# Gathering slot 1's plain rows between two pairs of stores, and opening its products ahead of the branch

## The chip, the cores and the metric

The kernel runs on one core of a Trainium2 chip. A core has five engines that run side by side: TensorE (PE in the profile, with its weight loads as PEld), VectorE (DVE), ScalarE (ACT), GpSimd (POOL) and SyncE (SP, used here for loads alone). Each engine works through its own list of instructions in order; semaphores make one wait for another. Transfers are issued by POOL (indirect ones, which gather or scatter rows by an index) and by SP, and run on 16 DMA engines. The metric is the device time of one execution, in microseconds (us).

## The reference

The program is chunked attention, followed by a mixture of experts with one expert per token.

```python
# q, k, v: (8, 8, 576, 64); chunks of 64 tokens attend within themselves
scores = scale * q_c @ k_c^T;  attn = softmax(scores);  out = attn @ v_c
x = out.transpose(0, 2, 1, 3).reshape(4608, 512)
# experts: w_gate (512, 8), w1 (8, 512, 1024), w2 (8, 1024, 512)
expert_idx = argmax(x @ w_gate);  gate_w = softmax(x @ w_gate)[expert_idx]
out[mask_e] = gate_w * (relu(x[mask_e] @ w1[e]) @ w2[e])     # for each expert e
```

## The kernel before, in words

The 4608 tokens are 36 tiles of 128 rows. A first part goes through 18 groups of two tiles: scores, softmax, attention output, the gate's logits, and the routing. Routing is done in seven batches of tiles (`BATCHES`, 6, 6, 6, 6, 4, 4, 4). For each batch it works out the place of every row in a scratch tensor in DRAM, `xd`, in which the rows of a batch lie together and are sorted by expert. `store` (line 420) sends each tile there with an indirect transfer on POOL's queue (line 427), through one of twelve views of `xd` that are declared disjoint from one another. A store can be given a tile `after`: then a copy of one column on ACT (line 425) holds it back until that tile is there.

The second part works through "slots". A slot is one expert with 256 plain rows and, by its kind, 0, 64 or 128 extra rows. The kind is only known at run time, so each slot from 1 on begins with a branch (line 1170): `form_a` (line 1116) takes plain rows alone, `form_x` (line 1135) takes extra rows too. A slot's first product is `gemm1` (line 644; matmuls at L616, 256 columns) or, with extra rows, `gemm1_x` (line 618; matmuls at L623, 320 or 384 columns), in eight blocks `f` of twelve matmuls, since each operand is split into a high and a low part and three products of these are summed over four chunks of 128. ACT takes the ReLU (L636, L627), DVE the low part (L641, L630). The second product (L693 to L695) sums three matmuls of 512 columns per block and half.

Rows come to a slot by a gather on POOL's queue, `rows_in` (line 548, the transfer at L550): two transfers of 128 plain rows (`gather`) and one of up to 128 extra rows (`gather_x`, into the tile `xg3`). The first two slots gather early, from the rows of the first batches alone: slot 0 from the first three batches (`TE[0]`, 18 tiles), slot 1 from the first six (`TE[1]`, 32 tiles). The extra rows of slot 1 come from all rows. Gathered rows are transposed on TensorE by `make_xt` (L572) and `make_xt_x` (L605), copied by ACT (L574, L607) and reduced to their low part by DVE (L575, L608).

The framework that builds the program orders any transfer that reads `xd` behind the writes to it that were issued before, and any write behind the reads that were issued before, unless a pair is declared free of dependence. The order of instructions on TensorE, DVE, ACT and POOL is the order in which the program writes them.

Slot 0 has no branch. It is cut into 32 half steps (`BLOCKS`, line 656, and `slot_0`), which `filler(n)` (line 680) hands out one by one between the last steps of the attention part; `halves[0]` counts how many are left, and one last call finishes the slot. At the end of the attention part (lines 1062 to 1093) a loop runs the routing of the last batches, the tables of all slots and a filler for as long as more than five halves are left, and stores one tile per turn. Behind it stand the remaining stores, `gather(1)`, `gather_x(1)`, two weight loads for slot 2 (`load_w`, L532), the fillers up to the last two halves, `make_xt(1)` and the last two halves with slot 0's end. Then each engine loads the kind from memory (L1191, L1193, L1200) and takes the branch of slot 1.

In `form_x` of the slots from 2 on, `FILL` (21) tiny matmuls of eight columns stand between the transposes of the extra rows and the first block. At the start of the program `WARM` (36) matmuls of ones (line 138) run while the first loads are under way. `bank` hands out PSUM banks: "S" alternates between two.

Of the kernel before, what the change touches and what calls it, by code (L numbers as in the profile page):

```python
# [8 lines left out]
F32 = mybir.dt.float32  # L9
F32R = mybir.dt.float32r  # L10
# [8 lines left out]
P = 128  # L19
# [18 lines left out]
NU = SMAX + 2  # L38
XW = D + 16
HB = 3  # L40
WARM = 36
FILL = 21
BIG = 1.0e6

# [2 lines left out]
def attn_moe_kernel(ctx: ExitStack, tc: tile.TileContext, q, k, v, wg, w, out):  # L47
# [50 lines left out]
    def bank(tag, shape):  # L98
        n = 1
        for x in shape[1:]:  # L100
            n *= x
        if tag == "S":
            t = psum[0].tile([P, 512], F32, name="psS", tag="S", bufs=2)
        else:
            t = slots[tag][turns[tag] % len(slots[tag])]
            turns[tag] += 1
        t = t[0:shape[0], 0:n]
        if len(shape) == 3:
            t = t.rearrange("p (a b) -> p a b", b=shape[2])
        return t  # L110
# [22 lines left out]
    ones = const.tile([P, P], BF16, name="ones")  # L133
    nc.vector.memset(ones, 1.0)

    pw = bank("U", [P, P])
    for _ in range(WARM):
        nc.tensor.matmul(pw, ones, ones, start=True, stop=True)
    iota_i = xg[0][0][:, 0:P].bitcast(I32)
    nc.gpsimd.iota(iota_i, pattern=[[1, P]], base=0, channel_multiplier=0)  # L140
    pid_i = xg[0][1][:, 0:NTILE].bitcast(I32)
# [146 lines left out]
        return px  # L288

    stored = set()  # L290

    def x_out(g, px, ri, xt):
        r0 = g * G % RB
# [126 lines left out]
    def store(n, after=None):  # L420

        for k, (b, i, t, di) in enumerate(waiting[:n]):
            x = xb[t // RB % XB][:, t % RB, :]
            if k == 0 and after is not None:
                nc.scalar.copy(x[:, XW - 1:XW], after)
            stored.add(t)
            nc.gpsimd.indirect_dma_start(  # L427
                out=xds[b % 2 * NMAX + i],
                out_offset=bass.IndirectOffsetOnAxis(ap=di[:, i, :], axis=0),
                in_=x, in_offset=None, bounds_check=NT - 1, oob_is_err=False)  # L430
        del waiting[:n]

    active = []
# [113 lines left out]

    def rows_in(t, u, h):
        rows = TE[u] * P if u < 2 and h < 2 else NT
        nc.gpsimd.indirect_dma_start(  # L550
            out=t[:, :], out_offset=None, in_=xd[0:rows, :],
            in_offset=bass.IndirectOffsetOnAxis(ap=place(u, h), axis=0),
            bounds_check=rows - 1, oob_is_err=False)

    def gather(u):
        for h in range(2):
            rows_in(rows_of(u)[h], u, h)
# [53 lines left out]
    def gemm1_pe(par, f, ph, part=range(4)):  # L611
        for kc in part:
            wh = w_hi[par][kc][:, f * 128:(f + 1) * 128]
            wl = w_lo[par][kc][:, f * 128:(f + 1) * 128]
            for i, (a, b) in enumerate(((wh, xhi), (wh, xlo), (wl, xhi))):
                nc.tensor.matmul(ph, a, b[:, kc, 0:BLK], start=kc + i == 0, stop=kc + i == 5)  # L616

    def gemm1_x(par, f, n, hh=None, hl=None):

# [60 lines left out]
    def filler(n):  # L680
        for _ in range(n):
            next(fill, None)
            halves[0] -= 1
# [378 lines left out]
    while active:  # L1062
        for x in "cat":
            advance(x)
        small_op(2)
        pauses()
        side_op(3)
        if halves[0] > 5:
            filler(1)
        if h0:  # L1070
            store(1, h0[-1][0][:, 0:1].bitcast(F32))
    store(NMAX)
    assert len(stored) == NTILE
    gather(1)
    gather_x(1)
    load_w(2, 0)
    load_w(2, 1)
# [10 lines left out]
    xT = y01.rearrange("p a (k t) -> p (a k) t", t=BLK)  # L1088
    hx = ctx.enter_context(tc.tile_pool(name="hx", bufs=HB))
    hq = ctx.enter_context(tc.tile_pool(name="hq", bufs=1))  # L1090
    filler(halves[0] - 2)
    make_xt(1, banks="QK")
    filler(3)
    def slot(u, kd, nxt):
        par = wset(u)
        py = [bank("UV"[m], [P, D]) for m in range(2)]
        if u > 1:
            spread(u + 1)

        last = [[hq.tile([P, BLK], F32R, name=f"{x}{f}") for x in ("hh", "hl")] for f in (6, 7)]  # L1100

        def block(f, h, ms=(0, 1)):
            for m in ms:
                gemm2(par, f, h, m, py)

        def later():

            if u == 1:
                yield from places()
            yield from find_u(u + 3)  # L1110

        def some(x, n):
            for _ in range(n):
                next(x, None)

        def form_a():
            h = []
            x = later()
            for f in range(8):
                h.append(gemm1(par, f, *(last[f - 6] if f > 5 else ())))  # L1120
                if f == 4 and u + 1 < SMAX:

                    tc.mark_branch_hint_location(f"kind{u + 1}", hint=(nxt + 1) >> 1, engines=PE)
                if f == 0 and u > 1:
                    gather_x(u + 1)
                if f == 5 and u > 1:
                    turn()
                    gather(u + 2)
                if f < 7:
                    split_step(u, f)  # L1130
                    some(x, 4 if u == 1 else 1)
                if f > 1:
                    block(f - 2, h[f - 2])

        def form_x(n):

            make_xt_x(u, n)
            pe = bank("K", [n, D])
            if u > 1:
                for _ in range(FILL):  # L1140
                    nc.tensor.matmul(pe[:, 0:8], ones[:, 0:n], ones[:, 0:8], start=True, stop=True)
            h = []
            x = later()

            def more(f):
                gemm2_pe(par, f, *h[f][1], pe)

            for f in range(8):
                h.append(gemm1_x(par, f, n, *(last[f - 6] if f > 5 else ())))
                if f == 4 and u + 1 < SMAX:  # L1150
                    tc.mark_branch_hint_location(f"kind{u + 1}", hint=(nxt + 1) >> 1, engines=PE)
                if f == 0 and u > 1:
                    gather_x(u + 1)
                if f == 5 and u > 1:
                    turn()
                    gather(u + 2)
                if f < 7:
                    split_step(u, f)
                    some(x, 4 if u == 1 else 1)
                if 1 < f < 7:  # L1160
                    block(f - 2, h[f - 2][0])
                    more(f - 2)
            more(5)
            more(6)
            block(5, h[5][0], (0,))
            more(7)
            finish(u, 2, pe, n)
            block(5, h[5][0], (1,))

        with tc.If(kd > 0, label=f"kind{u}") as c:  # L1170
            with tc.If(kd < 2) as c2:
                form_x(EXT // 2)
            with c2.Else():
                form_x(EXT)
        with c.Else():
            form_a()

        nc.gpsimd.drain()
        if u == 1:
            make_xt(u + 1)  # L1180
        else:
            make_xs()
        split_chunk(wset(u + 1), 5)
        for m in range(2):
            for f in (6, 7):
                block(f, last[f - 6], (m,))
            finish(u, m, py[m], on_act=m == 0)

        load_w(u + 2, 2)
# [48 lines left out]
```

## Time and profile before

| | us |
|---|---|
| median of 3 runs | 613.2 |
| lowest and highest | 611.22, 613.5 |
| the profiled execution | 611.45 |
| its span in the trace | 609.7 |

| engine | busy, us | share of the span |
|---|---|---|
| PE | 571.2 | 94% |
| PEld | 500.8 | 82% |
| DVE | 443.1 | 73% |
| ACT | 299.8 | 49% |
| POOL | 256.3 | 42% |

The profile shows one execution. A row of the timeline gives the start and the duration of an instruction (or of several alike), its engine, its line, what it writes and reads, and in brackets how long its engine had stood before it and what released it. A row of the chain gives start, duration and what was worked or waited on. A row of a stretch gives its bounds and length, then for each engine the busy time with the number of instructions in brackets, then the clock that was granted to TensorE (1.00 is full), the busy share of the DMA engines, and GB/s. "POOLq" and the like are the engines' sequencers, which wait on semaphores and issue transfers.

### The profile page before, as it was taken

The numbers are of one execution on the slowest core, as the hardware profiler recorded it, in microseconds if no ns is written. First come the engines' busy times: TensorE is split into PE (matmuls) and PEld (weight loads), VectorE is DVE, ScalarE is ACT, GpSimd is POOL, SyncE is SP. The second block draws the span as 40 slices with busy tenths as digits, with TensorE's granted clock in tenths as the row PEclk, the third lists the DMA queues.
The fourth block names the chain that finished last, engine by engine and source line by source line (L and its number), as shares of the span: only waits on it lengthen the run. The fifth ranks groups of instructions, "written<-read, shape, count | busy, mean of one in ns | idle before, by whom it ended". The sixth has DMA issues, their size and how long they took to land.

```text
span 609.7 us, 14951 instructions
## 1 busy us (share of the span) xinstructions
PE 571.2 (94%) x5710; PEld 500.8 (82%) x5710; DVE 443.1 (73%) x830; ACT 299.8 (49%) x560; POOL 256.3 (42%) x277
## 2 busy tenths in 40 slices
PE   7788879889899999999999989999999999999994
PEld 5566757678699999988788879999998899899893
DVE  6677979987555677776667658778756878878774
ACT  1465656663133545544345435555535555555552
POOL 2113545547524354425253325426432553454252
PEclk9898999999889999999999999999999999999998
DMA  8999999625566263256226512257652235632021
GB/s 282 356 348 309 354 328 308 216 86 197 183 227 204 77 208 109 73 188 217 60 63 223 200 40 81 72 192 275 203 161 85 59 105 198 207 90 82 20 56 37
DMA packets 59875, 103.29 MB, mean 169 GB/s; under 512 B 16416, under 2 KB 32800, under 8 KB 56160
## 3 DMA queue, kind: packets, MB, share of 16 engines
q0 software_dynamic: 20880, 60.74, 29.3%
q1 hardware_dynamic: 38864, 40.94, 21.1%
q8 instruction: 66, 1.08, 0.7%
q14 instruction: 65, 0.53, 0.3%
HBM read 122.65 MB, written 19.96 MB: 234 GB/s over the span
## 4 chain that ended last, share of the span: by engine, by line
PE 80%; DMA 6%; DVE 5%; issue 5%; ACT 2%; POOL 1%; SPq 1%; POOLq 0%; DVEq 0%; ACTq 0%
PE psS L616 18%; PE psS L623 8%; PE psL L616 6%; PE psU L693 5%; PE psU L694 5%; PE psV L693 5%; PE psU L695 5%; PE psV L694 5%; PE psV L695 5%; DMA out_y<-y,oid 3%; PE psL L623 3%; PE psU L286 2%; PE psS L232 2%; PE psT L309 2%; PE psL L321 1%
## 5 line engine op out<-in xcount | busy, mean ns | idle before, releaser
L77 DVE TENSOR_TENSOR wlo<-raw,whi 128x1024 fp32r<-128x1024 f32 x134 | 163.8, 1222 | 26.6 <-ACT whi L76 24.2
L76 ACT CAST whi<-raw 128x1024 fp32r<-128x1024 f32 x134 | 140.2, 1046 | 0.1
L532 POOL DMA_INDIRECT raw<-in_w,widx x71 | 78.8, 1109 | 124.0 <-DVE wlo L77 54.5
L636 ACT ACTIVATE hh<-psS 128x256 fp32r<-128x256 f32 x110 | 42.5, 386 | 174.1 <-PE psS L616 115.1
L616 PE MATMUL psS<-xhi,whi 128*128 128x256 f32 x344 | 97.6, 284 | 1.4 <-PE psV L695 1.2
L616 PE MATMUL psS<-xlo,whi 128*128 128x256 f32 x344 | 97.4, 283 | 0.3 <-DVE xlo L575 0.3
L616 PE MATMUL psS<-xhi,wlo 128*128 128x256 f32 x344 | 97.3, 283 | 0.0
L703 POOL DMA_INDIRECT out_y<-y,oid x40 | 46.8, 1171 | 115.5 <-ACT y L700 32.2
L641 DVE SCALAR_TENSOR_TENSOR hl<-psS,hh 128x256 fp32r<-128x256 f32 x110 | 46.4, 422 | 63.5 <-ACT xh L627 31.8
L550 POOL DMA_INDIRECT xg<-xd,idx x58 | 65.7, 1132 | 21.6 <-issue 18.4
L616 PEld LDWEIGHTS psS<-xhi,whi 128*128 128x128 f32 x344 | 65.7, 191 | 5.8 <-issue 2.4
L616 PEld LDWEIGHTS psS<-xlo,whi 128*128 128x128 f32 x344 | 65.7, 191 | 3.1 <-DVE xlo L575 0.5
L616 PEld LDWEIGHTS psS<-xhi,wlo 128*128 128x128 f32 x344 | 65.7, 191 | 0.0
L693 PE MATMUL psU<-whi,hh 128*128 128x512 f32 x144 | 57.6, 400 | 2.5 <-issue 1.3
L694 PE MATMUL psU<-wlo,hh 128*128 128x512 f32 x144 | 57.2, 397 | 0.0
L693 PE MATMUL psV<-whi,hh 128*128 128x512 f32 x144 | 56.9, 395 | 0.0
L694 PE MATMUL psV<-wlo,hh 128*128 128x512 f32 x144 | 56.7, 394 | 0.0
L695 PE MATMUL psU<-whi,hl 128*128 128x512 f32 x144 | 56.4, 392 | 0.0
L695 PE MATMUL psV<-whi,hl 128*128 128x512 f32 x144 | 56.4, 391 | 0.0
L84 POOL TENSOR_TENSOR wlo<-raw,whi 128x512 fp32r<-128x512 f32 x16 | 20.3, 1271 | 66.2 <-ACT whi L83 55.7
L427 POOL DMA_INDIRECT xd<-xb,di x32 | 32.3, 1008 | 14.7 <-issue 4.4
L594 DVE STREAM_TRANSPOSE y<-xg 128x1024 f32<-128x1024 f32 x16 | 33.1, 2070 | 0.6
(236 smaller groups left out, 1198.2 us busy)
## 6 DMA issues: line engine op xcount, KB each, us to landing
kb<-in_k SPq DMA_DIRECT2D x36, 256.0 KB
qt<-in_q SPq DMA_DIRECT2D x36, 256.0 KB
vb<-in_v SPq DMA_DIRECT2D x36, 256.0 KB
xg<-xg SPq DMA_DIRECT2D x256, 32.0 KB
raw<-in_w SPq DMA_DIRECT2D x16, 256.0 KB
raw<-in_w,widx POOLq DMA_INDIRECT x71
xg<-xd,idx POOLq DMA_INDIRECT x58
out_y<-y,oid POOLq DMA_INDIRECT x40
```

The costliest lines, as they stand in the source:

```text
L76: nc.scalar.copy(hi, src)
L77: nc.vector.tensor_tensor(lo, src, hi.bitcast(F32), ALU.subtract)
L532: nc.gpsimd.indirect_dma_start(out=raw[c][:, :], out_offset=None, in_=w, in_offset=bass.IndirectOffsetOnAxis(ap=widx[:, u, c:c + 1], axis= ...
L550: nc.gpsimd.indirect_dma_start(out=t[:, :], out_offset=None, in_=xd[0:rows, :], in_offset=bass.IndirectOffsetOnAxis(ap=place(u, h), axis=0 ...
L616: nc.tensor.matmul(ph, a, b[:, kc, 0:BLK], start=kc + i == 0, stop=kc + i == 5)
L623: nc.tensor.matmul(ph, a[par][kc][:, f * 128:(f + 1) * 128], b[:, kc, 0:BLK + n], start=kc + i == 0, stop=kc + i == 5)
L636: nc.scalar.activation(hh, ph, AF.Relu)
L641: nc.vector.scalar_tensor_tensor(hl, ph, 0.0, hh.bitcast(F32), ALU.max, ALU.subtract)
L693: nc.tensor.matmul(py, hh, wh, start=f == 0, stop=False)
L694: nc.tensor.matmul(py, hh, wl, start=False, stop=False)
L695: nc.tensor.matmul(py, hl, wh, start=False, stop=f == 7)
L703: nc.gpsimd.indirect_dma_start(out=outs[m], out_offset=bass.IndirectOffsetOnAxis(ap=oid[u % 3][0:n, m:m + 1], axis=0), in_=y, in_offset=No ...
```

## The change

Four things are changed. The warm-up is done with 9 matmuls of 512 columns in place of 36 of 128. The loop at the end of the attention part no longer stores tiles of the last batch; behind the loop all but the last two tiles are stored, then `gather(1)` is issued, then the last two tiles are stored, without the ACT copy; `gather(1)` is declared free of dependence on those stores of the last batch that were issued before it. One more half of slot 0 stands behind `make_xt(1)`. And slot 1's blocks 0 and 1 of the plain rows (`ahead`, two calls of `gemm1`) are issued ahead of the branch; in `form_x` their extra rows then have a product of their own, `gemm1_xx`, with 64 or 128 columns. `form_a` of slot 1 gets 27 of the tiny matmuls at its start, which the other form already has in the later slots and still lacks in slot 1.

```diff
-WARM = 36
+WARM = 9
...
-    pw = bank("U", [P, P])
+    pw = bank("U", [P, 4, P])
     for _ in range(WARM):
-        nc.tensor.matmul(pw, ones, ones, start=True, stop=True)
+        nc.tensor.matmul(pw, ones, ones.unsqueeze(1).broadcast_to([P, 4, P]), start=True, stop=True)
...
     stored = set()
+    late = []
...
-            nc.gpsimd.indirect_dma_start(
+            s = nc.gpsimd.indirect_dma_start(
                 out=xds[b % 2 * NMAX + i],
                 out_offset=bass.IndirectOffsetOnAxis(ap=di[:, i, :], axis=0),
                 in_=x, in_offset=None, bounds_check=NT - 1, oob_is_err=False)
+            if t >= TE[1]:
+                late.append(s)
...
     def rows_in(t, u, h):
         rows = TE[u] * P if u < 2 and h < 2 else NT
-        nc.gpsimd.indirect_dma_start(
+        g = nc.gpsimd.indirect_dma_start(
             out=t[:, :], out_offset=None, in_=xd[0:rows, :],
             in_offset=bass.IndirectOffsetOnAxis(ap=place(u, h), axis=0),
             bounds_check=rows - 1, oob_is_err=False)
+        if u == 1 and h < 2:
+
+            for s in late:
+                tc.declare_no_dep(g.ins, s.ins, reason="these rows lie behind the ones gathered")
...
+    def gemm1_xx(par, f, n):
+
+        ph = bank("S", [P, n])
+        for i, (a, b) in enumerate(((w_hi, xhi), (w_lo, xhi), (w_hi, xlo))):
+            for kc in range(4):
+                nc.tensor.matmul(ph, a[par][kc][:, f * 128:(f + 1) * 128], b[:, kc, BLK:BLK + n],
+                                 start=kc + i == 0, stop=kc + i == 5)
+        xh = hx.tile([P, EXT], F32R, name="xh")[:, 0:n]
+        nc.scalar.activation(xh, ph, AF.Relu)
+        xl = hx.tile([P, EXT], F32R, name="xl")[:, 0:n]
+        nc.vector.scalar_tensor_tensor(xl, ph, 0.0, xh.bitcast(F32), ALU.max, ALU.subtract)
+        return xh, xl
...
-        if h0:
+        if h0 and waiting and waiting[0][0] < NBAT - 1:
             store(1, h0[-1][0][:, 0:1].bitcast(F32))
-    store(NMAX)
+    store(len(waiting) - 2)
+    gather(1)
+    store(2)
     assert len(stored) == NTILE
-    gather(1)
     gather_x(1)
     load_w(2, 0)
     load_w(2, 1)
...
-    filler(halves[0] - 2)
+    filler(halves[0] - 3)
     make_xt(1, banks="QK")
-    filler(3)
+    filler(4)
...
+        ahead = [gemm1(par, f) for f in range(2)] if u == 1 else []
...
+        def fill_up(to, n):
+
+            for _ in range(n):
+                nc.tensor.matmul(to[:, 0:8], ones[:, 0:to.shape[0]], ones[:, 0:8], start=True, stop=True)
+
         def form_a():
+            if u == 1:
+                fill_up(bank("K", [P, D]), 27)
...
-                h.append(gemm1(par, f, *(last[f - 6] if f > 5 else ())))
+                h.append(ahead[f] if f < len(ahead) else gemm1(par, f, *(last[f - 6] if f > 5 else ())))
...
             if u > 1:
-                for _ in range(FILL):
-                    nc.tensor.matmul(pe[:, 0:8], ones[:, 0:n], ones[:, 0:8], start=True, stop=True)
+                fill_up(pe, FILL)
...
-                h.append(gemm1_x(par, f, n, *(last[f - 6] if f > 5 else ())))
+                h.append((ahead[f], gemm1_xx(par, f, n)) if f < len(ahead)
+                         else gemm1_x(par, f, n, *(last[f - 6] if f > 5 else ())))
```

## The prediction

> **What bounds the kernel now.** I read the page's head and its chain first, then TensorE's instructions in order of time, the granted clock in short stretches, and last POOL's instructions and the chain around the first branch.
>
> ```profile
> span 609.7 us, 14951 instructions
> PE 571.2 (94%) x5710; PEld 500.8 (82%) x5710; DVE 443.1 (73%) x830; ACT 299.8 (49%) x560; POOL 256.3 (42%) x277
> PE 80%; DMA 6%; DVE 5%; issue 5%; ACT 2%; POOL 1%; SPq 1%; POOLq 0%; DVEq 0%; ACTq 0%
> ```
>
> TensorE is busy for 94% of the span and 80% of the chain that ended last. A change pays if it takes away time in which TensorE stands, or in which it runs at a low clock. The change works at one such place, the passage from slot 0 to slot 1.
>
> ```profile
> 159.14 0.39 PE L693 MATMUL psV<-whi,hh 128*128 128x512 f32 x1
> ...
> 161.40 0.75 PE L572 MATMUL psQ<-ident,xg 128*128 128x128 f32 x4 [1.42 <-DMA xg<-xd,idx]
> 163.12 1.13 PE L572 MATMUL psK<-ident,xg 128*128 128x128 f32 x4 [0.97 <-DMA xg<-xd,idx]
> ...
> 168.34 1.65 PE L623 MATMUL psS<-xhi,whi 128*128 128x384 f32 x4 [0.68 <-ACT xhi L607]
> ...
> 174.61 0.85 PE L623 MATMUL psL<-xhi,whi 128*128 128x384 f32 x4
> ```
>
> TensorE waits 1.42 us for the first gather of slot 1, 0.97 us for the second and 0.68 us for ACT's copy of the transposed extra rows: 3.07 us. The arm taken is the one with 128 extra rows (384 columns at L623). The start of its third block, 174.61, is the mark against which I sum, since nothing behind it is changed.
>
> ```profile
> 53.19:56.60 3.41, 1.69 (x39) 1.59 (x32) 3.38 (x5) 0.44 (x5) 2.74 (x6) 1.00 1.02 358
> 83.90:87.32 3.42, 1.96 (x15) 1.58 (x15) 2.45 (x7) 1.30 (x3) 1.63 (x3) 1.00 1.00 332
> 159.00:162.41 3.41, 1.73 (x9) 1.04 (x7) 0.00 (x0) 0.22 (x1) 2.54 (x3) 1.00 0.50 120
> 162.41:165.82 3.41, 2.70 (x9) 2.32 (x10) 1.73 (x7) 0.95 (x2) 1.46 (x2) 0.50 0.78 250
> 165.82:169.24 3.42, 2.74 (x10) 2.05 (x9) 1.98 (x4) 0.59 (x1) 2.03 (x2) 0.50 0.99 395
> 169.24:172.66 3.42, 3.42 (x12) 3.42 (x11) 0.15 (x3) 0.02 (x1) 1.18 (x2) 0.50 0.52 201
> 172.66:176.07 3.41, 3.41 (x21) 3.41 (x21) 1.94 (x9) 1.09 (x4) 0.88 (x1) 1.00 0.92 288
> ```
>
> Here the second number is TensorE's busy time and the third from the end the granted clock. The clock changes on a grid of 3.41 us. After a stretch with 1.73 us of work (159.00) it is halved; a stretch with 1.96 us (83.90) was held. It comes back only behind a full stretch (3.42, from 169.24): 2.70 and 2.74 us were too little. So three stretches run at half clock, and their 2.70 + 2.74 + 3.42 = 8.86 us of work cost about 4.4 us more than at full clock. With the 3.07 us of waits the passage loses 7.5 us, which is all that a perfect change could win here.
>
> **What the change does, part by part.** *The warm-up.* 36 products of 128 columns become 9 of 512, the same 4608 columns.
>
> ```profile
> 1.05 4.02 PE L138 MATMUL psU<-ones 128*128 128x128 bf16 x36 [1.05 <-DVE ones L134]
> ...
> 7.28 0.69 PE L232 MATMUL psS<-kb,qt 64*64 64x64 f32 x32 [1.31 <-DMA qt<-in_q]
> ```
>
> They end at 5.07, and the scores then stand for a load until 7.28. Up to 2 us in the length of the warm-up are covered by that load: nothing, and without this cover 4.02 us at most.
>
> *The stores and the gathers on POOL's queue.* Before, the four stores of the last batch go first, then both plain gathers, the extra one and the weight loads.
>
> ```profile
> 149.74 0.98 POOL L427 DMA_INDIRECT xd<-xb,di  x1 [0.15 <-POOL xb L406]
> 151.03 1.37 POOL L427 DMA_INDIRECT xd<-xb,di  x1 [0.30 <-issue]
> 152.70 0.97 POOL L427 DMA_INDIRECT xd<-xb,di  x1 [0.30 <-issue]
> 153.98 1.20 POOL L427 DMA_INDIRECT xd<-xb,di  x1 [0.30 <-issue]
> 157.92 1.04 POOL L550 DMA_INDIRECT xg<-xd,idx  x1 [2.74 <-PE psS L616]
> 159.26 1.01 POOL L550 DMA_INDIRECT xg<-xd,idx  x1 [0.30 <-issue]
> 160.58 1.00 POOL L550 DMA_INDIRECT xg<-xd,idx  x1 [0.30 <-issue]
> 161.88 0.99 POOL L532 DMA_INDIRECT raw<-in_w,widx  x1 [0.30 <-issue]
> ```
>
> After, the order is store, store, gather, gather, store, store, extra gather, loads. The gathers no longer wait for the last batch, so the first takes about the place of the third store: 152.8, and the second 154.15 (1.34 us apart, as 157.92 and 159.26).
>
> ```profile
> 153.98 2.97 DMA xd<-xb,di
> ...
> 159.26 3.81 DMA xg<-xd,idx
> ...
> 167.70 0.60 ACT xhi L607
> ...
> 174.77 2.08 PE psL L623 x12
> 176.85 0.23 PE psU L693
> ```
>
> They land 3.48 us (157.92 to 161.40) and 3.81 us behind their starts, at 156.3 and 157.96, ahead of TensorE's need at 159.14. Both waits, 2.39 us, go.
>
> What is late next: the two stores behind the gathers. The edit frees each gather of the stores already in the list `late`; the two stores that are issued afterwards write the same scratch tensor that the gathers read, and nothing frees them. The trace shows such a pair, slot 0's gathers and the store behind them.
>
> ```profile
> 118.21 1.05 POOL L550 DMA_INDIRECT xg<-xd,idx  x1 [0.16 <-PE psT L277]
> 119.56 1.01 POOL L550 DMA_INDIRECT xg<-xd,idx  x1 [0.30 <-PE psT L309]
> ...
> 124.17 1.05 POOL L427 DMA_INDIRECT xd<-xg,di  x1 [3.16 <-DVE xb L298]
> ```
>
> ```profile
> L427 POOLq EVENT_SEMAPHORE  x2: 43/43/43, 121.8 to 123.4; - x2
> ```
>
> That store's two semaphore waits end at 121.8 and 123.4, which is 3.6 and 3.8 us behind the starts of the two gathers, their landing; the store starts 0.75 us later. The releaser that the row names, L298, I put down to chance. So the third store starts at 157.96 + 0.75 = 158.7 and the fourth at 160.0 (1.28 later, as 152.70 and 153.98). It lands at 162.97 (2.97). The extra gather, which reads all rows, waits for it and starts 0.97 later (156.95 to 157.92) at 163.9. It lands 3.5 to 3.8 us on; I take 167.5. Queued behind on POOL are the loads for slot 2, at 165.2 in place of 161.88. Their data are first needed behind the third block, past 174, which covers 3.4 us; uncovered they would cost those 3.4 us.
>
> The four one-column ACT copies that paced these stores go away; ACT is not what TensorE waits for there, so nothing.
>
> *The order on TensorE.* One more half of slot 0 (three products of 512 columns) lies behind the transposes, and two blocks of slot 1's plain rows go ahead of the branch.
>
> ```profile
> 139.24 0.60 PE L309 MATMUL psT<-ident,xb 128*128 128x128 f32 x4
> 139.68 0.60 PE L309 MATMUL psQ<-ident,xb 128*128 128x128 f32 x4
> 140.12 0.51 PE L931 MATMUL psL<-sel_g,lp 128*128 128x8 f32 x4
> ...
> 164.91 0.69 DVE L575 TENSOR_TENSOR xlo<-psK,xhi 128x512 fp32r<-128x512 f32 x1 [1.28 <-ACT xhi L574]
> ...
> 204.92 2.87 PE psS L616 x24
> ```
>
> From 159.14: eight transposes at full clock 0.88 (139.24 to 140.12), to 160.02; three halves of 3 x 0.23, 2.07, to 162.09. Under these halves ACT makes two copies (0.60 each) and DVE two differences (0.69 each), done near 161.8: no wait. Two plain blocks take 2.87 (204.92), to 164.96. TensorE's sequencer crosses the branch under these 2.87 us of products; uncovered it would at first only eat into the wait that follows. Then TensorE stands until 167.5, for 2.5 us; transposes 0.6, ACT's copy with its hand-over 0.66 (as now): 168.8.
>
> Then come the extra rows of the two blocks, 24 products of 128 columns. No row shows this shape. From below, a third of 384 columns is 0.058 us each (2.08 for 12), 1.4 in all; from above, as much as 256 columns, 0.12 each, 2.9. I take 0.11, the spacing of the 128-column transposes above, which load as large a weight for as few columns: 2.64, to 171.4. (So splitting the two blocks costs 2.87 + 2.64 against 2 x 2.08 = 4.16, that is 1.35 us more work.) By the Trainium skill, TensorE: Matmul & The Clock Gate, section LDWEIGHTS, a weight load takes its columns divided by 1.2 GHz, an estimate of 107 ns however short the product; by it the split would be 0.1 us cheaper. No run here shows it for this shape.
>
> *The clock.* The waits of 2.5 and 0.66 us lie within 3.8 us. For nearly every position of the grid one stretch of 3.41 us then holds under 1.73 us of work, and the clock is halved. It returns behind one full stretch, or two where the first is partly idle. Stepping the grid through its positions, with the clock halved behind less than 1.9 us of work (between 1.73 and 1.96) and given back behind a stretch with less than 0.5 us of idle time, the loss behind 168.8 is 1.4 to 3.1 us, 2.2 in the mean. The third block then starts at 173.6, against 174.61.
>
> **Sum.** Waits 3.07 - 3.16 = -0.1; half clock 4.4 - 2.2 = 2.2 gained; more work -1.35; and 0.25 that these terms leave open of the 15.47 us from 159.14 to 174.61 before: a gain of 1.0 us. The profiled execution took 611.45 us, 1.75 over its span; it becomes 610.45. The median of the three runs, 613.2, lies 1.75 above it; the same gain gives **612.2 us**. As behind the mark TensorE runs on without a break for most of the time, the shift passes to the end.
>
> **The rivals.** 0.5% of the time, 3.1 us, is about what a measurement of this kernel can tell from no change.
>
> *A, the forecast:* the last two stores wait for the gathers, TensorE waits for the extra rows and cools. 612.2, own range 610.2 to 614.6 (the ends of the half-clock loss, of the 24 products, and grids on which the kernel before loses less than the 10.2 us at half clock seen here). Chance 0.60.
>
> *B, the stores are not held.* Then they start at 155.5 and 156.8, the fourth lands at 159.8, the extra gather starts at 160.7 and lands by 164.5, before 164.96. Only 0.66 us of wait stays, the clock holds, the third block starts at 168.9, and the gain is 5.7: 607.5. For it: the edit says that the rows lie apart, and the row of the store at 124.17 names L298, a write to another tile, as its releaser. Against it: the semaphore rows. Chance 0.14.
>
> *C, the clock holds in spite of the wait.* Then 171.4, a gain of 3.2: 610.0. For it: 1.96 us of work in a stretch held the clock. Against it: 1.73 did not, and there the longest single wait was 1.42 us, shorter than the new one. The Trainium skill, same page, section Why this matters for your kernels, asks only that no gap exceed about 3 us; by that rule the 2.5 us would be harmless and C the outcome, but the trace, with the clock halved at 162.41 behind 1.42 us and a part of the next wait, speaks against it. Chance 0.12.
>
> *D, slower: the narrow products don't bring the clock back.* They give TensorE 128 columns in 0.11 us where a plain block gives it 256 in 0.12. If a stretch of them counts as too little work, as 2.70 us did, they run at half clock for all of 5.3 us, and one or two stretches behind them too: a loss of 2.64 + 1.7 = 4.3 to 2.64 + 3.4 = 6.0 in place of 2.2. The mark moves to 175.7 or 177.4, and the time to 614.3 or 616.0. It decides from a half-clock loss of 3.2 us on. For it: two stretches with four fifths of work stayed at half clock. Against it: the scores' small products (L232) do not cool it. Chance 0.14.
>
> **How the numbers follow.** Faster by over 0.5%: all of B, three quarters of C, 0.04 of A: 0.27. Slower by over 0.5%: about half of D and 0.03 of A: 0.10. The rest, 0.63, is within 0.5%. The range holds A and C whole, B at its edge and the lower part of D: 607.4 to 615.2.
>
> **What the profile will show.** Right: the first gathers start near 152.8 and 154.2, the next store near 158.7, the extra gather near 163.9; TensorE has no wait for the plain rows, two blocks of L616 end near 165.0, and a wait of about 2.5 us for the extra gather follows; the 24 narrow products are 0.11 us apart at full clock; the clock is halved once, for one or two stretches. The prediction is wrong if the third store starts near 155.5 (B), if the granted clock stays at 1.00 through the wait (C), or if the narrow products and what follows run at 0.50 for over two stretches (D); and in its size if the extra gather lands a microsecond earlier or later, for each such microsecond moves the mark by as much and can decide over the clock.

## The result, and the profile after

| | before | after |
|---|---|---|
| median, us (22 runs each) | 614.42 | 619.15 |
| lowest and highest, us | 610.32, 622.03 | 616.11, 623.5 |
| ratio after to before | | 1.0087 [1.0063, 1.0112] |
| profiled execution, us | 611.45 | 616.83 |

The change made the kernel slower by 0.87%, some 5.3 us (0.0087 x 614.42), where 612.2 us was forecast, with a chance of 0.63 for a difference within 0.5%. Here and below the median is over all executions of a run, while a ratio leaves out those that are more than 1.5% above the fastest of their kernel, which changes a reading for the cut kernels alone. The head of the page of after:

```profile
span 615.0 us, 14931 instructions
PE 578.0 (94%) x5707; PEld 503.6 (82%) x5707; DVE 440.6 (72%) x830; ACT 298.6 (49%) x556; POOL 265.3 (43%) x277
```

TensorE is busy for 6.8 us more (571.2 before) at the same share, so the clock and the waits are the places to look, not another engine. In POOL's instructions of after (start, duration, line; in brackets the idle time ahead and what ended it) the order and the hold are as forecast, 2 to 3 us later:

```profile
154.18 0.97 POOL L428 DMA_INDIRECT xd<-xb,di  x1 [0.30 <-issue]
155.46 1.05 POOL L553 DMA_INDIRECT xg<-xd,idx  x1 [0.30 <-issue]
156.81 1.01 POOL L553 DMA_INDIRECT xg<-xd,idx  x1 [0.30 <-issue]
161.05 1.02 POOL L428 DMA_INDIRECT xd<-xb,di  x1 [3.24 <-DMA xg<-xd,idx]
162.38 1.00 POOL L428 DMA_INDIRECT xd<-xb,di  x1 [0.31 <-issue]
165.96 1.05 POOL L553 DMA_INDIRECT xg<-xd,idx  x1 [2.58 <-DVE o_b L893]
```

The third store stands 3.24 us for the gathers, and the extra gather starts at 165.96. TensorE in the passage (L579 are the transposes of slot 1's plain rows, L612 of the extra rows, L630 the narrow products, L643 the third block):

```profile
168.90 0.63 PE L579 MATMUL psQ<-ident,xg 128*128 128x128 f32 x4
...
174.80 0.65 PE L612 MATMUL psT<-ident,xg 128*128 128x128 f32 x4
...
176.46 0.67 PE L630 MATMUL psS<-xhi,whi 128*128 128x128 f32 x4 [1.01 <-ACT xhi L614]
...
179.20 0.91 PE L643 MATMUL psL<-xhi,whi 128*128 128x384 f32 x4
```

The mark, the third block, is 4.6 us later than before (174.61). But here nothing waits for the extra rows: the plain transposes themselves start only at 168.90, where 159.14 was assumed. The reason stands in ACT's instructions ahead of them, and in the stretches of the clock (length, TensorE's busy time, and third from the end the granted clock):

```profile
152.02 0.18 ACT L411 ACTIVATE ce<-psK 128x8 f32<-128x8 f32 x1
158.97 0.66 ACT L656 ACTIVATE hh<-psS 128x256 fp32r<-128x256 f32 x2 [6.77 <-remote]
```

```profile
155.45:158.86 3.41, 1.73 (x5) 0.86 (x5) 0.00 (x0) 0.00 (x0) 2.05 (x2) 1.00 0.58 170
158.86:162.27 3.41, 2.40 (x11) 2.40 (x12) 2.65 (x11) 0.66 (x2) 1.02 (x1) 0.50 0.08 27
```

ACT does nothing for 6.77 us, though the products that it is to take were ready (the first of them ended near 151). TensorE has four stops of 0.28 to 0.84 us in that time for which the trace names no releaser, and then stands 1.29 us for what follows ACT. This came in this one execution: in the 17 other traces that reach slot 1, ACT never stands for over 2.5 us in the 20 us ahead of its transposes, and two of them (f2 and w2) are of the same kernel and slower than before all the same. So it can't be what makes 22 runs slower. A single profile would have led to the wrong cause here; the experiments had to tell.

### The profile page after: what moved, and what is told of

Read it like the earlier page. It is cut to its first block, busy times and chain, and to the rows that moved or that the text cites. A ratio compares the mean times of both kernels' runs of the same rounds, so it can differ in the third digit from the quotient of the medians.

```text
span 615.0 us, 14931 instructions
## 1 busy us (share of the span) xinstructions
PE 578.0 (94%) x5707; PEld 503.6 (82%) x5707; DVE 440.6 (72%) x830; ACT 298.6 (49%) x556; POOL 265.3 (43%) x277
## 5 line engine op out<-in xcount | busy, mean ns | idle before, releaser
L535 POOL DMA_INDIRECT raw<-in_w,widx x71 | 84.6, 1191 | 121.2 <-DVE wlo L77 39.9
L623 PE MATMUL psS<-xhi,whi 128*128 128x256 f32 x352 | 100.8, 286 | 2.4 <-DVE hl L661 1.3
L623 PE MATMUL psS<-xlo,whi 128*128 128x256 f32 x352 | 100.3, 285 | 0.3 <-DVE xlo L582 0.3
L623 PE MATMUL psS<-xhi,wlo 128*128 128x256 f32 x352 | 100.2, 285 | 0.3 <-issue 0.3
L553 POOL DMA_INDIRECT xg<-xd,idx x58 | 68.3, 1178 | 25.3 <-issue 21.9
L623 PEld LDWEIGHTS psS<-xhi,whi 128*128 128x128 f32 x352 | 67.9, 193 | 7.9 <-issue 2.5
L623 PEld LDWEIGHTS psS<-xlo,whi 128*128 128x128 f32 x352 | 67.9, 193 | 3.2 <-DVE xlo L582 0.5
L623 PEld LDWEIGHTS psS<-xhi,wlo 128*128 128x128 f32 x352 | 67.9, 193 | 0.5 <-issue 0.5
```

What stands on the lines that cost most here:

```text
L535: nc.gpsimd.indirect_dma_start(out=raw[c][:, :], out_offset=None, in_=w, in_offset=bass.IndirectOffsetOnAxis(ap=widx[:, u, c:c + 1], axis= ...
L553: g = nc.gpsimd.indirect_dma_start(out=t[:, :], out_offset=None, in_=xd[0:rows, :], in_offset=bass.IndirectOffsetOnAxis(ap=place(u, h), ax ...
```

## The experiments

All kernels were run next to the kernel before; each ratio is to that, with its 95% interval. The four cut kernels are not in the table. "Passage" is from slot 0's transposes to slot 2's (before: 129.39 to 201.07, 71.68 us), "half clock" the time at 0.50 inside it.

| run | stores held by the gathers | median, us | ratio | passage, us | half clock, us |
|---|---|---|---|---|---|
| the kernel after, as above | yes | 619.15 | 1.0087 [1.0063, 1.0112] | 74.68 | 6.83 |
| f2, the kernel after | yes | 613.39 | 1.0051 [1.0020, 1.0082] | 68.60 | 0 |
| w2, the kernel after | yes | 615.63 | 1.0079 [1.0055, 1.0104] | 73.34 | 10.24 |
| f4, old warm-up, instructions level | yes | 614.04 | 1.0061 [1.0029, 1.0094] | 68.77 | 0 |
| e2, old warm-up | yes | 618.36 | 1.0100 [1.0052, 1.0148] | 73.47 | 10.24 |
| e4, no blocks ahead | yes | 616.25 | 1.0070 [1.0030, 1.0111] | 73.83 | 6.83 |
| w1, narrow products made wide | yes | 612.89 | 1.0044 [1.0011, 1.0076] | 70.46 | 3.41 |
| h1, the wait filled with products | yes | 611.15 | 1.0014 [0.9987, 1.0041] | 68.87 | 0 |
| h3, stores freed | no | 610.80 | 1.0013 [0.9982, 1.0045] | 67.51 | 0 |
| h6, stores freed, no blocks ahead | no | 612.73 | 1.0013 [0.9979, 1.0048] | 70.45 | 3.41 |
| e3, stores first | no | 613.21 | 1.0011 [0.9977, 1.0046] | 71.88 | 6.83 |
| f3, stores first, no blocks ahead | no | 610.21 | 0.9999 [0.9972, 1.0025] | 66.90 | 0 |
| e1, before with the new warm-up | as before | 614.76 | 1.0047 [1.0014, 1.0080] | 69.34 | 3.41 |
| f1, the same, instructions level | as before | 610.80 | 1.0000 [0.9968, 1.0033] | 69.78 | 0 |
| h5, the kernel before | as before | 612.19 | 1.0028 [0.9999, 1.0058] | 69.38 | 0 |

h5 sets the scale: two equal kernels came out 0.28% apart, so no single difference below that is read. Passage and half clock are of one execution each.

**The warm-up (e1, e2, f1, f4).** e1 puts the new warm-up alone into the kernel before, e2 puts the old one back into the kernel after:

```diff
-WARM = 9
+WARM = 36
...
-    pw = bank("U", [P, 4, P])
+    pw = bank("U", [P, P])
     for _ in range(WARM):
-        nc.tensor.matmul(pw, ones, ones.unsqueeze(1).broadcast_to([P, 4, P]), start=True, stop=True)
+        nc.tensor.matmul(pw, ones, ones, start=True, stop=True)
```

> The kernel before with the new warm-up alone (9 products of 512 columns for 36 of 128). Theory 1 (the loss lies ahead of slot 1's passage and comes from TensorE's instruction stream being 27 products shorter from the start, so that every later instruction lies elsewhere in the blocks in which instructions are fetched): slower than before by 5 to 10 us, ratio 1.008 to 1.016; slot 0's transposes near 131.6 in place of 129.39 and the start of slot 1's transposes near 166 to 169 in place of 160. Theory 2 (the loss comes from the stores and gathers moved on POOL's queue, or the ACT copies taken away): ratio 1.000 within 0.003. Theory 3 (it comes from the blocks put ahead of the branch): ratio 1.000 within 0.003.

> The kernel after with the old warm-up back, all the rest kept. Theory 1: the passage keeps its gain of about 5 us and the loss ahead of it goes: ratio to before 0.990 to 0.995, slot 0's transposes near 129.4 and slot 1's third block near 169. Theories 2 and 3: as the kernel after, ratio 1.006 to 1.011.

The warm-up alone cost 0.47%, less than theory 1 asked for and more than the other two allow; but with the old one back the kernel after was no faster (1.0100). The two then differ in how many instructions stand ahead of all later ones. f1 adds 27 tiny products to e1's warm-up, f4 takes the 27 out of `form_a` of e2, so that both have the number of the kernel before:

```diff
+    for _ in range(27):
+        nc.tensor.matmul(pw[:, 0, 0:8], ones, ones[:, 0:8], start=True, stop=True)
```

> The kernel before with the new warm-up and 27 tiny products of 8 columns behind it, so that TensorE has as many instructions as before and all later ones lie where they lay. If the warm-up alone costs time because the later instructions lie elsewhere (theory 1): ratio to before 1.000 within 0.003. If it costs by its own length or shape: as the run with the new warm-up alone, 1.003 to 1.008.

> The kernel after with the old warm-up, and without the 27 tiny products in the arm that is not taken, so that all instructions behind the arms lie where they lay in the kernel before. Theory H: as the kernel after, ratio 1.006 to 1.011. Theory 1 (the warm-up's shift ahead of the passage costs 3 us): 1.001 to 1.006.

f1 is at 1.0000, f4 with 1.0061 where the kernel after is (1.0051 in f2, run beside it). So the new warm-up costs nothing where the later instructions keep their place, and it is not what made the kernel after slower. Theory 1 falls as the cause; that the place of the instructions is what cost e1 its 0.47% is argued from f1 alone, and the intervals of the two overlap.

**The hold, and the blocks ahead (e3, e4, f2, f3).** e3 stores all four tiles first and leaves the gathers freed; e4 takes out the two blocks ahead of the branch; f3 does both; f2 is the kernel after again.

```diff
-    store(len(waiting) - 2)
+    store(len(waiting))
     gather(1)
-    store(2)
```

```diff
-        ahead = [gemm1(par, f) for f in range(2)] if u == 1 else []
+        ahead = []
```

> The kernel after with all four last stores ahead of the two gathers, which stay freed of them, so that no store is held by a gather. Theory 1: as the kernel after within 0.003 (ratio 1.006 to 1.011), since nothing waited for the held stores there. Theory 2: if the gathers' place between the stores costs the time ahead of the passage, 5 to 10 us faster than the kernel after, ratio 0.993 to 1.001; if the missing ACT copies cost it, as the kernel after. Theory 3: as the kernel after.

> The kernel after without the two blocks ahead of the branch (slot 1 computes all its blocks 384 columns wide again). Theory 1: the time ahead of the passage stays as in the kernel after (slot 1's transposes near 169), and the passage loses 0.5 to 3 us for the wait for the extra rows that the two blocks covered, less 1.3 us for narrow products that are gone: ratio to before 1.006 to 1.013. Theory 2: the same. Theory 3: ratio 1.000 or below.

> The kernel after once more. Theory H (the hold: the last two stores wait for the gathers, the extra gather comes late, TensorE stands about 2 us for it and then runs two to three stretches at half clock): ratio 1.006 to 1.011, ACT without its stop of 6.8 us near 152 to 159 (an accident of that execution), a wait of about 2 us for the extra rows, the third block 14.5 to 16 us behind the start of slot 1's transposes. If the stop of ACT belongs to the kernel, it is there again.

> All four last stores ahead of the freed gathers, and no blocks ahead of the branch: all blocks 384 columns wide. Theory H: neither the hold nor the wait is there, TensorE has no gap over 0.7 us in the passage, the clock stays, and the third block starts 9 to 11 us behind the start of slot 1's transposes (15.5 before): 4 to 6 us faster than before, ratio 0.990 to 0.994. Theory 3 (the blocks ahead cost nothing of their own): the same as the run with the stores first and the blocks ahead, 1.001.

Theory 3 falls with e4: without the blocks ahead it is still 0.70% slower. With the stores first the loss is gone, with the blocks ahead (1.0011) and without them (0.9999). f2, the kernel after, is at 1.0051, a little under the 1.006 expected; ACT's long stop is not there, and TensorE stands for the extra rows:

```profile
165.55 0.75 PE L612 MATMUL psT<-ident,xg 128*128 128x128 f32 x4 [1.51 <-DMA xg<-xd,idx]
```

But in f2's trace the clock held, so the third block starts 11.73 us behind slot 1's transposes and not 14.5 to 16. f3 was expected to win 4 to 6 us and won nothing, though its passage is 3.1 us shorter than the mean of the four traces with the stores and gathers of before (70.0); that stays open. In e3 TensorE stops in the narrow products behind the branch, and the trace names no releaser:

```profile
172.15 0.90 PE L630 MATMUL psS<-xlo,whi 128*128 128x128 f32 x3 [1.89 <-issue]
```

That is not of e3 alone: the kernel before has such a stop in slot 1's second block where it keeps its clock (1.31 us in f1, 1.22 in h5).

**Cut kernels (c0, c1).** To see where along the program the time is lost, both kernels were cut behind slot 0 and behind slot 1, so that these times are of parts of the computation.

> The kernel before cut behind slot 0: slot 1 and all later slots, the extra gather of slot 1 and the weight loads for slot 2 are left out; the stores and the two plain gathers stay. It measures the part ahead of the passage alone, near 167 us (slot 0 ends near 161 in the profile, then the scaling and the store of its rows), run after run. Only its difference to the kernel after cut at the same place counts.

> The kernel after cut behind slot 0 in the same way. Theory H (all of the loss is in the passage: the wait for the extra rows and the half clock behind it): as the kernel before cut there, within 1 us. Theory U (the part ahead of the passage got slower, as the profiles with slot 0's transposes at 130.5 to 136 hint against 129.4 before): 2 to 5 us longer.

> The kernel before cut behind slot 1 (slots 2 and later are left out, everything up to slot 1's last products, stores and the weight loads issued there is kept): near 215 us. Only its difference to the kernel after cut there counts.

> The kernel after cut behind slot 1. Theory H: 3 to 5 us longer than the kernel before cut there, with none of it ahead of the passage. Theory U: the same 3 to 5 us here, and 2 to 5 of them already in the pair cut behind slot 0. Theory L (the loss comes behind slot 1, from the later weight loads): within 1 us of the kernel before cut there.

By the medians, all executions counted, behind slot 0: 166.8 us before (163.49 to 167.74, 7) against 167.64 after (165.24 to 170.81, 6); behind slot 1: 219.59 (215.95 to 221.42, 7) against 219.27 (218.8 to 221.63, 5). By the ratios, which are to the whole kernel before (610.6 us), it looks otherwise: 0.2681 [0.2666, 0.2696] against 0.2720 [0.2702, 0.2738] behind slot 0 and 0.3542 [0.3522, 0.3561] against 0.3609 [0.3589, 0.3630] behind slot 1, which is 2.4 and 4.1 us longer and what theory U says. But they rest on 3 executions against 3 and 3 against 5, picked by a line through a spread of some 4 us that is as large as what was looked for. So the cut kernels are inconclusive, with a hint at theory U. The spread shows in the other traces too, where slot 0's transposes start between 128.22 and 136.18 in kernels with the change and between 129.29 and 132.39 in those without, and at 135.63 in the kernel before cut behind slot 1.

**The hold alone (h3, h6), and its wait filled (h1).** h3 keeps the order on POOL and frees the last stores of the gathers as well, which makes rival B real; h6 takes out the blocks ahead too. h1 keeps the hold and has TensorE do 7 products on the ones where it would stand.

```diff
-    late = []
+    late, early_g = [], []
...
             if t >= TE[1]:
                 late.append(s)
+                for g in early_g:
+                    tc.declare_no_dep(s.ins, g.ins, reason="these rows lie behind the ones gathered")
...
         if u == 1 and h < 2:
+            early_g.append(g)
```

```diff
-                fill_up(bank("K", [P, D]), 27)
+                fill_up(bank("K", [P, D]), 13)
...
+            pe = bank("K", [n, D])
+            if u == 1:
+                for _ in range(7):
+                    nc.tensor.matmul(pe.rearrange("p (a t) -> p a t", t=P), ones[:, 0:n], ones.unsqueeze(1).broadcast_to([P, 4, P]), start=True, stop=True)
             make_xt_x(u, n)
-            pe = bank("K", [n, D])
```

> The kernel after with the last two stores freed of the gathers as well, so that the order on POOL stays and only the hold goes (rival B made real). Theory H: the third store starts about 1.3 us behind the second gather, the extra gather about 160 to 161 on the old time axis, TensorE's wait for the extra rows is under 0.5 us, and the ratio to before falls to 0.990 to 1.002, 3 to 6 us below the kernel after. If the order itself (the gathers between the stores) is the cost: as the kernel after, 1.005 to 1.009.

> The same without the two blocks ahead of the branch. Theory H: no wait for plain rows, at most 1 us for the extra ones, no half clock in the passage: ratio 0.990 to 1.000. If the freed order costs by itself: 1.005 to 1.009.

> The kernel after with the hold, and 7 products of 512 columns on the ones (1.6 us, their result is not used) where TensorE stands for the extra rows; 14 of the tiny products in the arm not taken are left out, so that later instructions lie where they lay. If the half clock behind the wait is what the hold costs: the passage stays at full clock in most executions, ratio 0.997 to 1.003. If the hold costs by something else (later weight loads, the wait itself): as the kernel after, 1.005 to 1.009.

> The kernel before once more: ratio 1.000 within 0.003. Its trace shows whether the wait for the two gathers (2.4 us) and the three stretches at half clock come in each execution; if the stretches are missing, the profile on which the prediction's 4.4 us for the half clock rested was one of the dear ones.

POOL's instructions of h3:

```profile
153.88 1.17 POOL L555 DMA_INDIRECT xg<-xd,idx  x1 [0.30 <-issue]
155.35 1.11 POOL L428 DMA_INDIRECT xd<-xb,di  x1 [0.30 <-issue]
156.77 1.00 POOL L428 DMA_INDIRECT xd<-xb,di  x1 [0.31 <-issue]
160.34 1.05 POOL L555 DMA_INDIRECT xg<-xd,idx  x1 [2.58 <-DMA xd<-xb,di]
```

The store starts 1.47 us behind the gather (4.24 in after), the extra gather at 160.34, close to the 160.7 forecast for rival B, and no wait for the extra rows is left. The ratio is 1.0013. In h6 TensorE, without the blocks ahead, still stands 2.00 us for the extra rows (1 us at most was expected) and has one stretch at half clock; its ratio is 1.0013 all the same. h1 keeps the hold, as the third store's wait of 3.05 us shows, but not TensorE's idle time:

```profile
164.84 1.69 PE L1169 MATMUL psK<-ones 128*128 128x512 bf16 x7
166.81 0.75 PE L612 MATMUL psT<-ident,xg 128*128 128x128 f32 x4 [0.29 <-DMA xg<-xd,idx]
168.23 0.66 PE L630 MATMUL psS<-xhi,whi 128*128 128x128 f32 x4 [0.68 <-ACT xhi L614]
...
170.97 0.92 PE L643 MATMUL psL<-xhi,whi 128*128 128x384 f32 x4
```

It takes no wait away, since the products take as long as TensorE stood; and still the ratio is 1.0014. Its interval lies apart from those of w2 and of the result, but overlaps with that of f2. So the order of the transfers is not the cost, nor the time for which the extra rows are late, nor the later weight loads behind them: it is that TensorE stands there. What is left is what standing does to the clock.

**Why the half clock is dear here (w1, w2).** w1 makes the 24 narrow products 256 columns wide; w2 is the kernel after beside it.

```diff
-        ph = bank("S", [P, n])
+        pw = bank("S", [P, BLK])
+        ph = pw[:, BLK - n:BLK]
-                nc.tensor.matmul(ph, a[par][kc][:, f * 128:(f + 1) * 128], b[:, kc, BLK:BLK + n],
+                nc.tensor.matmul(pw, a[par][kc][:, f * 128:(f + 1) * 128], b[:, kc, n:BLK + n],
```

> The kernel after with the extra rows' 24 products of the first two blocks computed over 256 columns (the second half of the plain rows along with the 128 extra ones; the plain part is thrown away, the result is the same). 24 products of 0.12 in place of 0.114 us: 0.15 us more at full clock. If it is the narrow products that don't bring the clock back (rival D): where the clock is halved it is for one or two stretches, none of them a full one without return, and the ratio falls to 1.002 to 1.005. If their width doesn't matter: as the kernel after, 1.005 to 1.010.

> The kernel after once more, beside the run with the wide products: ratio to before 1.005 to 1.009; if its trace has the clock halved in the passage, for two to three stretches, with a full stretch of narrow products that stays at half.

TensorE's instructions of w2, and its clock stretch by stretch:

```profile
159.87 0.63 PE L579 MATMUL psQ<-ident,xg 128*128 128x128 f32 x4
...
167.88 1.13 PE L612 MATMUL psT<-ident,xg 128*128 128x128 f32 x4 [1.94 <-DMA xg<-xd,idx]
...
169.68 1.12 PE L630 MATMUL psS<-xhi,whi 128*128 128x128 f32 x4 [0.68 <-ACT xhi L614]
...
174.86 1.59 PE L643 MATMUL psL<-xhi,whi 128*128 128x384 f32 x4
...
203.48 0.63 PE L579 MATMUL psT<-ident,xg 128*128 128x128 f32 x4
```

```profile
164.57:167.98 3.41, 1.47 (x13) 1.26 (x12) 0.85 (x2) 0.73 (x2) 2.51 (x3) 1.00 0.49 125
167.98:171.39 3.41, 2.73 (x12) 2.33 (x13) 0.82 (x3) 0.58 (x1) 2.79 (x3) 0.50 1.00 329
171.39:174.81 3.42, 3.42 (x18) 3.42 (x18) 0.99 (x5) 0.28 (x1) 1.30 (x2) 0.50 0.92 326
174.81:178.22 3.41, 3.41 (x13) 3.41 (x13) 1.49 (x5) 0.28 (x1) 0.00 (x0) 0.50 1.03 428
```

The wait of 1.94 us leaves 1.47 us of work in a stretch, and the clock is halved. The stretch from 171.39 holds nothing but narrow products, without a gap, and the clock does not return; only behind the stretch from 174.81, which holds the third block, is it back. 2.73 + 3.42 + 3.41 = 9.56 us of work at half clock cost 4.8 us. Two more traces have such a stretch, e2 with narrow products up to 180.97 and the kernel after cut behind slot 1 with narrow ones up to 171.63:

```profile
177.65:181.07 3.42, 3.42 (x18) 3.42 (x17) 0.98 (x5) 0.28 (x1) 1.54 (x2) 0.50 0.90 298
168.86:172.27 3.41, 3.41 (x17) 3.41 (x17) 1.07 (x6) 0.55 (x2) 2.24 (x2) 0.50 0.85 258
```

Both are followed by another at half clock. The stretches of w1:

```profile
165.08:168.49 3.41, 1.55 (x10) 1.36 (x11) 1.13 (x4) 0.58 (x1) 2.49 (x4) 1.00 0.90 260
168.49:171.91 3.42, 3.42 (x18) 3.42 (x17) 0.98 (x5) 0.28 (x1) 2.61 (x3) 0.50 0.96 309
171.91:175.32 3.41, 3.41 (x20) 3.24 (x20) 1.74 (x6) 0.99 (x4) 0.00 (x0) 1.00 1.00 394
```

Halved in the same way (1.55), but one full stretch of wide products brings the clock back: 3.41 us at half in place of 10.24, and a passage of 70.46 against 73.34. Of the two stretches that w1 is spared, one is due to the width. The other is the first of w2, which has a gap of 0.68 us in it and would not have been full with wide products either; that is where the grid fell. By this reading the narrow products' own part in w2 is one stretch, 1.7 us of the 4.8. The ratios (1.0044 and 1.0079) go the same way, with intervals that overlap.

**The clock of the timed executions.** A trace shows one execution, but every timed one has its mean granted clock on record. One minus this clock, times the span, is the most that half clock can have cost it. The means over the executions that count for the ratio:

| run | lost to the clock, us | before, beside it | difference | measured loss, us |
|---|---|---|---|---|
| w2, the kernel after | 13.2 | 8.9 | 4.3 | 4.8 |
| f2, the kernel after | 11.6 | 10.0 | 1.6 | 3.1 |
| f4, old warm-up, instructions level | 13.0 | 10.0 | 3.0 | 3.7 |
| e2, old warm-up | 15.5 | 11.3 | 4.2 | 6.1 |
| e4, no blocks ahead | 12.3 | 11.3 | 1.0 | 4.3 |
| w1, narrow products made wide | 9.4 | 8.9 | 0.5 | 2.7 |
| h1, the wait filled | 9.4 | 9.0 | 0.4 | 0.9 |
| h3, stores freed | 11.1 | 9.0 | 2.1 | 0.8 |
| h5, the kernel before | 10.7 | 9.0 | 1.7 | 1.7 |

The measured loss is the ratio less one, times the median of the kernel before. In the five runs left out here (e1, e3, f1, f3, h6) the difference lies between 1.2 us less than before and 0.8 more. By h5 a difference is good to some 2 us. In w2, f4 and e2 the clock can account for most of the loss, and in h1 its extra loss is gone. In f2, e4 and w1 it accounts for about half or less, and the rest was not found. These means don't say where in the program the clock was low.

## Why the prediction was wrong

**Right:** POOL's queue. With the passage of w2 starting 0.73 us later than forecast (159.87 for 159.14): second gather 154.77 (154.15 forecast), third store 158.91 (158.7), extra gather 164.02 (163.9), its rows there at 167.88 (167.5). The wait is 1.94 us (2.5), ACT's hand-over 0.68 (0.66). The 24 narrow products take 2.74 us at full clock (176.46 to 179.20 in after) against 2.64. Their 0.114 us each fits, to 7%, the estimate of 107 ns from the Trainium skill, TensorE: Matmul & The Clock Gate, section LDWEIGHTS. The plain rows are no longer waited for.

**The failed step: the term of the half clock, on both sides of the sum.** It was entered as 4.4 us before less 2.2 after, a gain of 2.2. By the mean clock of the timed executions, over the whole program, it is a loss of 1.6 us in f2 and 4.3 in w2.

On the side of before, 4.4 us was the price of one execution, and was taken for that of the kernel. Three more traces of the same passage (f1, e1, h5) have 0, 3.41 and 0 us at half clock, for waits as long. h5:

```profile
164.35 0.75 PE L572 MATMUL psQ<-ident,xg 128*128 128x128 f32 x4 [1.38 <-DMA xg<-xd,idx]
...
166.16 0.75 PE L572 MATMUL psK<-ident,xg 128*128 128x128 f32 x4 [1.05 <-DMA xg<-xd,idx]
...
169.63 0.96 PE L623 MATMUL psS<-xhi,whi 128*128 128x384 f32 x4 [0.68 <-ACT xhi L607]
```

```profile
161.60:165.03 3.43, 2.05 (x11) 1.36 (x9) 0.00 (x0) 0.00 (x0) 2.51 (x4) 1.00 0.40 106
165.03:168.44 3.41, 2.36 (x13) 1.76 (x13) 1.70 (x7) 1.17 (x2) 1.87 (x2) 1.00 0.85 232
```

Here the grid splits the two waits so that 2.05 and 2.36 us of work stay, and the clock holds. From the end of the 29 halves to the mark these kernels take 15.47 (on record), 13.57, 13.13 and 13.17 us, 13.8 in the mean: 1.6 us of the forecast gain were only the bad draw of one profile. The saving from a held clock is also smaller than 4.4 us, since f1 and h5 then have the stop without a releaser of 1.31 and 1.22 us. For after the grid was stepped through its positions; for before it was not, although the range of the forecast names such executions.

On the side of after, "It returns behind one full stretch" was read from a stretch of wide products and applied to narrow ones. It fails there, so that in the executions of w2 and e2 the 2.2 us became 4.8; in those of f2 and f4 they became nothing, since the clock held. By the Trainium skill, same page, section Part 1: The HAM clock gate (the "warmup" mystery), one sustained busy window of about 3.4 us brings the full clock back; w2, e2 and the kernel after cut behind slot 1 each have such a window, full by the profile, behind which it did not. That page's remark that the window runs free of the kernel fits the spread between executions of one kernel.

**A second step fell with it:** "nothing behind it is changed", said of the mark. In w2 the half clock reaches past the mark, and from there to slot 2's transposes it takes 28.62 us (174.86 to 203.48) against 26.46 in all four traces of before. Without half clock, in f2, it is 27.11: of the 0.65 us more, 0.09 lie in the third block and the rest in two short stops in the last halves ahead of slot 2's transposes, whose cause is open. The sum had nothing for them.

**The sum again,** from the end of 29 halves to slot 2's transposes: 13.8 + 26.46 = 40.3 us before in the mean of four traces. Where the clock is halved, w2 has 14.99 + 28.62 = 43.6 and e2 43.7, 3.3 us more; where it holds, f2 has 38.8 and f4 39.0, 1.4 us less. The mean of these four is 41.3, only 1.0 us more. They are no fair sample: the profiles of f2 and f4, at 606.86 and 608.15 us, are the shortest of their 12 executions each, and that of e2, at 626.07, the longest of its 7. Measured were 3.1 us in the session of f2 (0.0051 x 610.62), 4.8 in that of w2 (0.0079 x 610.72) and 5.3 at first. If nearly every execution is halved, the passage gives the 3.3 us, and what is above is not accounted for; how many are is not known.

**The rivals.** D, with a chance of 0.14, is what happened in w2 and e2: the narrow products don't bring the clock back, with a half-clock loss of 4.3 to 6.0 forecast and 4.8 measured. Its times, 614.3 and 616.0, were still too low because they started from the dear profile of before, and from a median of three executions that was 1.2 us below that of 22 (613.2 and 614.42). B was not the kernel's behaviour, but h3, which makes it so, has its times on POOL's queue and not its 607.5. C is what f2 and f4 show, in one execution each. With the 1.6 us of the base added D's times are 615.9 and 617.6, and half of D would not have stood within 0.5%, nor the range have ended at 615.2.

**That the part ahead of 159.14 is unchanged** was assumed in the sum, and is neither shown nor refuted. The cut kernels hint at 2.4 us more there. The traces don't: slot 0's transposes start at 130.1 us in the mean of the four with the stores and gathers of before and at 130.5 in the mean of the twelve others that are not cut, and from slot 2's transposes to the end the two groups take 410.0 and 409.9 us. h1 and h3 share most of that part and are at 1.0014 and 1.0013; but their passages are 1.2 and 2.5 us shorter than the mean of before, so they leave room for a loss of 2 to 3 us elsewhere.

**Which version to take.** None beat the kernel before. h3 and f3, which win the passage (67.51 and 66.90 us), end at 1.0013 and 0.9999; where their 2 to 3 us go was not found.

## What to carry to other kernels

A loss that hangs on where a free-running grid falls has a price only as a mean over executions, for the kernel before as for the kernel after; one profile of before can put a gain into the sum that is nobody's. When a read is moved ahead of a write and freed of the writes issued earlier, look at the writes issued later: the hold only changes sides. And where TensorE must stand for about 2 us ahead of small products, wide products without use in that gap are worth a try: in h1 they kept the clock and cost nothing that could be measured.

## What the runs showed of the hardware

- A stretch of 3.4 us filled without a gap by 128-column products at half clock did not give the clock back (w2 from 171.39, e2 from 177.65 with 0.1 us of wider ones at its end); one filled by 256-column products did (w1 from 168.49), and one by 384-column ones (h6 from 169.76).
- TensorE's busy time in a stretch doesn't decide alone whether the clock is halved: 1.73 us led to half clock before, 1.76 us was held in f4 (163.01 to 166.42) and 1.90 in f2 (162.47 to 165.88), and in e3 a stretch with 2.35 us (167.90 to 171.31), mostly narrow products, was followed by half clock.
- 27 products fewer at the start of the program cost 0.47% in e1, and nothing once 27 tiny ones took their place (f1), with intervals that overlap.
- ACT stood for 6.77 us in one execution of after with its input ready; what it stood for the trace does not say.
